# Channel attention followed by a channel mix on one core: token stripes of four per partition, held stores, and the xk mix one step later

## The chip, the cores and the metric

The kernel runs on one core of a Trainium2 chip. The time is device microseconds (us) from one launch: the median of 11 runs of the kernel before is 508.24 us, the runs lie between 506.58 and 510.48 us. One more execution was recorded by the profiler; the views below are of that one.

The engines are named as in the profile: PE multiplies matrices, PEld loads its weights, DVE and ACT work element by element, POOL here mostly issues the casting DMAs, SP issues the other DMAs. In the trace each engine works through its instructions in the order of the program (only the weight loads of PE run ahead) and waits on semaphores for the others.

## The reference, cut to what matters

```
# B, N, C = 4, 6208, 256; d_ff = 1024; float32 in and out
qn = q / (norm(q, axis=1) + 1e-6);  kn = k / (norm(k, axis=1) + 1e-6)
a  = softmax(kn^T @ qn / tau)                # 256 x 256 for each batch
x  = v @ a                                   # 6208 x 256 for each batch
x_prev = x one token earlier (zeros before the first token)
xk = mu_k * x + (1 - mu_k) * x_prev
xr = mu_r * x + (1 - mu_r) * x_prev
out = sigmoid(xr @ w_r) * (relu(xk @ w_k) ** 2 @ w_v)
```

## The kernel before, in words

**Blocks.** Each batch has 12 blocks of M = 512 tokens (S = 4 slabs of P = 128), and 64 tokens left over; the four leftovers make one last small block. So there are 48 full blocks, numbered 0 to 47 over all batches, and block 48. Everything after `x` is kept transposed, channels on the partitions and tokens along the free axis: `xT` is 128 x 2 x 513 (two channel halves, 512 tokens, and one column ahead of them with the token before).

**Start.** q and k of batch 0 are read in 13 groups of float32 by DMAs from SP (`group_load`, L113), cast and multiplied (`cov_first`, L171) while they come in. Then the softmax of batch 0 follows, block 0 of v is transposed by PE (`v_transpose_pe`, L374), and `x_first` (L412) makes the first `xT`.

**Main loop** (L709 on). For block index i the loop runs eight steps j = 0 to 7. In one pass it does the upward product of block i+1 (`up`, L507: one of eight pieces in each step, two matmuls and a Relu on ACT that leaves `kr`), the squares `kk = kr*kr` on DVE (`square`, L521: pieces 0 to 3 in one instruction at j = 4, pieces 4 and 5 at j = 6, pieces 6 and 7 at j = 0 of the next pass), the downward product of block i (`down`, L529), its end (`finish`, L549: tanh on ACT, then a DVE product into `res`, for slabs 0 to 3 at j = 3, 5, 7 and 1), and it prepares block i+2: `x_half` at j = 0 and 2 (PE product, ACT cast into `xT`), `mix_delta` at j = 3, the two halves of `xk` at j = 4 and 5, and, for block i+1, the two halves of `xr` at j = 0 and 2 (`mix`, L495).

Within a step the order is: finish, one softmax piece, up, square, down, x_half and mixes, transposes, one unit of the next batch, one of its additions. There is no scheduler: this order is the order on every engine.

**The next batch.** Beside the blocks, the covariance of the following batch is built in units (`unit`, L650): a PE product and, for two units at a time, squares on ACT, added up on DVE by `pairs_add` and `quad_add` (L229 and L233, lines L231, L235, L247). There are six units in a block up to i = 7, then four or five, and none in the last 14 blocks. An addition is taken from the queue at j = 1, 6 or 7. When a batch is complete its softmax runs as a chain of pieces, one in each step (L348): `norms` sums with PE (L279), then `roots`, `pow2` on POOL, and `invert` (L307: four DVE instructions).

**DMAs.** v is read by POOL as bfloat16 (`v_load`, L360), six blocks ahead; apart from blocks 1 and 2 partition p gets tokens p, 128+p, 256+p and 384+p, in four runs of 1 KB. From block 4 on SP transposes it (`v_transpose`, L367), five blocks ahead. `res` (three buffers) is stored by SP when slab 3 is finished (L561), again in runs of 1 KB.

The lines about `xk`, word for word:

```
                if j == 3:
                    mix_delta(n)
                if j in (4, 5):
                    mix(n, "xk", int(j > 4))
```

Of the kernel before, what the change touches and what calls it, by code (L numbers as in the profile page):

```python
# [18 lines left out]
def kernel(  # L19
# [40 lines left out]
    half = const.tile([P, 4], F32, name="half")  # L60
    vT0 = const.tile([P, 2, M + 1], BF16, name="vT0")

# [16 lines left out]
    st_ps = {}  # L79
    adds = []  # L80
    sums = {}
    now = [0]
# [30 lines left out]
    def group_load(b, g):  # L113
        rows, n = rows_of(b, g)
        if b == 0:
            t_f = []
            for i, t in enumerate((q, k)):
                f = pq.tile([P, S, C], F32, name=f"f{i}", tag=f"f{i}", bufs=6)
                (nc.sync if g else nc.scalar).dma_start(f[:rows, :n], qk_src(t, b, g))  # L119
                t_f.append(f)  # L120
            groups[b, g] = tuple(t_f)
        else:
            qk = pq.tile([P, S, 2, C], BF16, name="qk", tag="qk", bufs=5)
            groups[b, g] = (qk,)
            for i, t in enumerate((q, k)):
                nc.gpsimd.dma_start(rows_at(qk, b, g, i)[:rows, :n], qk_src(t, b, g))  # L126
# [79 lines left out]
    def unit_square(b, g, s):  # L206

        rows, n = rows_of(b, g)
        if s % 2:
            return  # L210
        qk = groups[b, g][0]
        if n == 1:
            t = sums[b, "left"] = pq.tile([P, 1, 2 * C], BF16, name="sq", tag="sq1", bufs=2)
            nc.scalar.activation(t[:rows], qk[:rows].rearrange("p s i c -> p s (i c)")[:, :1], AF.Square)
            return
        if s == 0:
            sums[b, g] = pq.tile([P, S, 2 * C], BF16, name="sq4", tag=f"f{g % 2}", bufs=6)
        t = sums[b, g]
        to = t[:, s:s + 2].rearrange("p s (i c) -> p i s c", i=2)
        if apart(b, g):  # L220
            nc.scalar.activation(to, qk.rearrange("p s i c -> p (s i c)").rearrange(
                "p (i s c) -> p i s c", i=2, s=S)[:, :, s:s + 2], AF.Square)
        else:
            nc.scalar.activation(t[:, s:s + 2], qk[:, s:s + 2].rearrange("p s i c -> p s (i c)"), AF.Square)  # L224
        if s == 2:
            adds.append((now[0] + 2, b, lambda: pairs_add(b, g)))
            adds.append((now[0] + 3, b, lambda: quad_add(b, g)))
# [38 lines left out]
    def softmax_pieces(b):  # L266
# [70 lines left out]

        def weigh(ih):
            nc.scalar.activation(a_sb[:, b, ih, :], e_sb[:, ih], AF.Copy, scale=sm[:, ih:ih + 1])

# [11 lines left out]
    NBLK = len(blocks)  # L352
    L1 = L + 1
    xl = const.tile([P, 2, B, L1], BF16, name="xl")
    st = {}
# [4 lines left out]
    def v_load(i):  # L360
        b, t = blocks[i]
        v_bf = p2.tile([P, S, C], BF16, name="v_bf", tag="v_bf", bufs=6)
        nc.gpsimd.dma_start(v_bf, v[b, t * M:(t + 1) * M, :].rearrange(  # L363
            "(p s) c -> p s c" if i in (1, 2) else "(s p) c -> p s c", p=P))
        st[i, "v"] = v_bf
# [8 lines left out]
    def v_transpose_pe(i, evac):  # L374

        v_bf = st.pop((i, "v"))
        vT_ps = ps.tile([P, S, 2, P], BF16, name="vT_ps", tag="kT_ps", bufs=3)
        for s in range(S):
            for h in range(2):
                nc.tensor.transpose(vT_ps[:, s, h], v_bf[:, s, h * P:(h + 1) * P], ident)  # L380

        if i == 0:
            return lambda: evac(vT0[:, :, 1:].rearrange("c h (s p) -> c s h p", s=S), vT_ps)
        vT = p2.tile([P, S, 2, P], BF16, name="vT", tag="vT", bufs=5)
        st[i, "vT"] = vT
        if i == 3:
            return lambda: evac(vT, vT_ps)
        flat = vT.rearrange("c s h p -> c (s h p)")
        st[i, "vT"] = flat.rearrange("c (h s p) -> c s h p", h=2, s=S)
        return lambda: evac(flat.rearrange("c (h p s) -> c h p s", h=2, s=S),  # L390
                            vT_ps.rearrange("c s h p -> c h p s"))

    def x_half(i, dh):
        b, t = blocks[i]
        if dh == 0:
            xT = p2.tile([P, 2, M + 1], BF16, name="xT", tag="xT", bufs=3)
            st[i, "x"] = xT
            if t == 0:
                nc.vector.memset(xT[:, :, 0:1], 0.0)
            else:  # L400
                nc.scalar.copy(xT[:, :, 0:1], st[i - 1, "x"][:, :, M:M + 1])
        xT = st[i, "x"]
        vT = st[i, "vT"]
        xT_ps = ps.tile([P, M], F32, name="xT_ps", tag="xT_ps", bufs=2)
        for ih in range(2):
            nc.tensor.matmul(xT_ps, a_sb[:, b, ih, dh * P:(dh + 1) * P], vT[:, :, ih, :],  # L406
                             start=ih == 0, stop=ih == 1)
        nc.scalar.copy(xT[:, dh, 1:], xT_ps)  # L408

    H = M // 2  # L410

    def x_first():  # L412

        mix_tiles(0)
        xT = p2.tile([P, 2, M + 1], BF16, name="xT", tag="xT", bufs=3)
        st[0, "x"] = xT
        dv = st[0, "d"]
        pairs = st[0, "ps"] = []

        def difference(a):  # L420
            c = slice(a * H, (a + 1) * H)
            nc.vector.tensor_tensor(dv[:, :, c], vT0[:, :, a * H + 1:(a + 1) * H + 1], vT0[:, :, c], op=OP.subtract)

        def product(a, ih):
            if ih == 0:
                pairs.append([ps.tile([P, 2, H], F32, name="x_ps", tag=tag, bufs=bufs)
                              for tag, bufs in ((("vr_ps", 2), ("vr_ps", 2)), (("s_ps", 1), ("xT_ps", 2)))[a]])
            for t, src in zip(pairs[a], (vT0[:, ih, a * H + 1:(a + 1) * H + 1], dv[:, ih, a * H:(a + 1) * H])):
                for dh in range(2):
                    nc.tensor.matmul(t[:, dh], a_sb[:, 0, ih, dh * P:(dh + 1) * P], src,  # L430
                                     start=ih == 0 and dh == 0, stop=ih == 1, skip_group_check=True)
            if ih:
                for dh in (0, 1) if a == 0 else (slice(0, 2),):
                    nc.scalar.copy(xT[:, dh, a * H + 1:(a + 1) * H + 1], pairs[a][0][:, dh])
        return difference, product

    def mix_first(key, a, dh):

        c = slice(a * H, (a + 1) * H)
        m = less[:, dh:dh + 1] if key == "xk" else less[:, 2 + dh:3 + dh]  # L440
        nc.vector.scalar_tensor_tensor(st[0, key][:, dh, c], st[0, "ps"][a][1][:, dh], m,
                                       st[0, "x"][:, dh, a * H + 1:(a + 1) * H + 1], op0=OP.mult, op1=OP.add)

# [14 lines left out]
    def left_x(b):  # L458
# [18 lines left out]
        return go, go2  # L477

    def mix_tiles(i):
        st[i, "d"] = p2.tile([P, 2, M], BF16, name="delta", tag="delta", bufs=2)  # L480
# [3 lines left out]
    def mix_delta(i):  # L484
        mix_tiles(i)
        delta = st[i, "d"]
        if i < NBLK - 1:
            xT = st[i, "x"]
            nc.vector.tensor_tensor(delta, xT[:, :, 1:], xT[:, :, :M], op=OP.subtract)  # L489
        else:  # L490
# [4 lines left out]
    def mix(i, key, dh):  # L495
        mu = mu_k_t if key == "xk" else mu_r_t
        o = st[i, key]
        if i < NBLK - 1:
            nc.vector.scalar_tensor_tensor(o[:, dh], st[i, "d"][:, dh], mu[:, dh:dh + 1],  # L499
                                           st[i, "x"][:, dh, :M], op0=OP.mult, op1=OP.add)  # L500
        else:
# [27 lines left out]
    def down(i, j):  # L529
# [5 lines left out]
        if j == 0:  # L535
            st[i, "res"] = p2.tile([P, S, D], F32, name="res", tag="res", bufs=3)
        if h == 0:
# [11 lines left out]
    def finish(i, s):  # L549
# [7 lines left out]
        b, t = blocks[i]  # L557
        dst = out[b, t * M:(t + 1) * M, :].rearrange("(s p) c -> p s c", p=P)
        if i < NBLK - 2:
            if s == S - 1:  # L560
                nc.sync.dma_start(dst, res)  # L561
        elif s % 2:
# [3 lines left out]
    def last_block(i):  # L566
# [3 lines left out]
        SL = B * L // P  # L570
        res = p2.tile([P, S, D], F32, name="res", tag="res", bufs=3)
        r_ps = ps.tile([P, SL, D], F32, name="r_ps", tag="s_ps")
# [25 lines left out]
    nc.vector.memset(fill, 1.0)  # L598
    nc.vector.memset(vT0[:, :, 0:1], 0.0)

# [46 lines left out]
    NORMS = 13  # L647
    holds = [0]

    def unit(ahead=2):  # L650
# [58 lines left out]
    for i in range(-2, NBLK - 1):  # L709
        for j in range(8):  # L710
# [7 lines left out]
            if chain:  # L718
                piece = chain[0]
                if len(chain) == NORMS and any(e[1] == holds[0] for e in adds):  # L720
                    piece = None
# [20 lines left out]
            if 0 < i + 2 < NBLK:  # L742
# [4 lines left out]
                if j == 3:  # L747
                    mix_delta(n)
                if j in (4, 5):
                    mix(n, "xk", int(j > 4))  # L750

# [24 lines left out]
            if j in slots and pos["mm"] < len(units):  # L776
                unit()
            if adds and adds[0][0] <= now[0] and (j in (1, 6, 7) or adds[0][1] == holds[0] and chain):
                next_add()
            now[0] += 1  # L780
            if i >= 0 and i % NB == 2 and j == 1 and i // NB < B:
# [41 lines left out]
```

## Time and profile before

| | |
|---|---|
| median of 11 runs | 508.24 us |
| the profiled execution | 509.51 us |
| its span, first to last instruction | 507.6 us |
| PE, DVE, ACT busy | 479.5, 431.0, 428.5 us |
| granted PE clock, mean | 0.997 |
| DMA packets, bytes moved | 132694, 83.46 MB |

A row of a group gives the line, the engine, what is written and read, shape and count, then the busy time and the mean of one instruction in ns, and the idle time of the engine just before it with what ended it. A row of the timeline gives the start and the duration in us, then the engine, the line, the shapes, "x2" where two like instructions are merged, and in brackets the idle time before it and who ended it. On DVE the next instruction can start a little before the one ahead of it is over, so the distance from start to start, called pitch here, says how long an instruction holds the queue.

### The profile page before, as it was taken

The numbers are of one execution on the slowest core, as the hardware profiler recorded it, in microseconds if no ns is written. First come the engines' busy times: TensorE is split into PE (matmuls) and PEld (weight loads), VectorE is DVE, ScalarE is ACT, GpSimd is POOL, SyncE is SP. The second block draws the span as 40 slices with busy tenths as digits, with TensorE's granted clock in tenths as the row PEclk, the third lists the DMA queues.
The fourth block names the chain that finished last, engine by engine and source line by source line (L and its number), as shares of the span: only waits on it lengthen the run. The fifth ranks groups of instructions, "written<-read, shape, count | busy, mean of one in ns | idle before, by whom it ended". The sixth has DMA issues, their size and how long they took to land.

```text
span 507.6 us, 9206 instructions
## 1 busy us (share of the span) xinstructions
PE 479.5 (94%) x3370; PEld 331.3 (65%) x3429; DVE 431.0 (85%) x788; ACT 428.5 (84%) x869; POOL 96.4 (19%) x143
## 2 busy tenths in 40 slices
PE   3578999999899999999999999999999999999996
PEld 1345667767676676676776677667666666666675
DVE  3776899999889899899889989989988787878884
ACT  5767999989899898988999898888888878888784
POOL 0044342222133322212043231200031000000000
PEclk9998999999999999999999999999999999999999
DMA  8999999999999999997699999982297753452123
GB/s 322 410 313 195 197 167 199 194 176 201 217 163 167 191 177 180 154 191 121 122 204 148 181 187 198 153 158 71 63 190 126 128 122 104 87 90 79 48 77 105
DMA packets 132694, 83.46 MB, mean 164 GB/s; under 512 B 50660, under 2 KB 125736, under 8 KB 132648
## 3 DMA queue, kind: packets, MB, share of 16 engines
q0 software_dynamic: 55824, 33.01, 49.7%
q1 hardware_dynamic: 76504, 49.59, 42.7%
q8 instruction: 27, 0.44, 0.4%
q10 hardware_dynamic: 320, 0.26, 0.2%
q14 instruction: 19, 0.16, 0.1%
HBM read 78.71 MB, written 25.43 MB: 205 GB/s over the span
## 4 chain that ended last, share of the span: by engine, by line
PE 85%; DMA 7%; DVE 5%; ACT 1%; issue 1%; SPq 0%; POOL 0%; DVEq 0%; POOLq 0%
PE vr_ps L546 32%; PE kT_ps L514 29%; PE vr_ps L542 9%; PE xT_ps L406 7%; PE s_ps L263 6%; DMA f<-in_q_dram 6%; DMA v_bf<-in_v_dram 1%; DVE kk L527 1%; DVE xk L499 1%; PE x_ps L430 1%; DVE res L556 0%; DVE xr L499 0%; ACT xT L408 0%; DVE delta L489 0%; SPq L119 0%
## 5 line engine op out<-in xcount | busy, mean ns | idle before, releaser
L519 ACT ACTIVATE kr<-kT_ps 128x512 bf16<-128x512 f32 (+1 forms) x390 | 234.9, 604 | 35.7 <-PE kT_ps L514 30.0
L546 PE MATMUL vr_ps<-w_v_sb,kk 128*128 128x256 bf16 x1536 | 230.2, 273 | 0.4
L514 PE MATMUL kT_ps<-xk,w_k_sb 128*128 128x512 bf16 (+1 forms) x722 | 217.6, 377 | 0.3 <-DVE xk L499 0.2
L546 PEld LDWEIGHTS <-kk 128*128 128x128 bf16 x1536 | 150.3, 98 | 57.3
L527 DVE TENSOR_TENSOR kk<-kr 128x2048 bf16<-128x2048 bf16 (+1 forms) x148 | 125.6, 849 | 0.2 <-ACT kr L519 0.2
L556 DVE SCALAR_TENSOR_TENSOR res<-res,vr_ps 128x256 f32<-128x256 f32 x192 | 79.7, 415 | 51.8 <-ACT res L555 51.8
L514 PEld LDWEIGHTS <-w_k_sb 128*128 128x128 bf16 x780 | 75.5, 98 | 27.5 <-issue 0.6
L555 ACT ACTIVATE res<-vr_ps 128x256 f32<-128x256 f32 x192 | 76.6, 399 | 1.3 <-PE vr_ps L546 1.3
L542 PE MATMUL vr_ps<-w_r_sb,xr 128*128 128x256 bf16 x384 | 73.3, 273 | 2.5
L408 ACT CAST xT<-xT_ps 128x512 bf16<-128x512 f32 x94 | 55.8, 594 | 19.9 <-PE xT_ps L406 19.6
L499 DVE SCALAR_TENSOR_TENSOR xk<-delta,mu_t,xT 128x512 bf16<-128x512 bf16 x94 | 69.9, 745 | 0.0
L499 DVE SCALAR_TENSOR_TENSOR xr<-delta,mu_t,xT 128x512 bf16<-128x512 bf16 x94 | 69.9, 744 | 0.0
L542 PEld LDWEIGHTS <-xr 128*128 128x128 bf16 x384 | 37.6, 98 | 44.6 <-issue 0.2
L126 POOL DMA_DIRECT2D qk<-in_q_dram x39 | 26.1, 670 | 165.0 <-ACT kr L519 141.2
L406 PE MATMUL xT_ps<-vT,a_sb 128*128 128x512 bf16 x188 | 55.9, 379 | 0.0
L263 PE MATMUL s_ps<-qk 128*128 128x256 bf16 (+1 forms) x294 | 55.8, 273 | 0.0
L224 ACT ACTIVATE sq<-qk 128x1024 bf16<-128x1024 bf16 x48 | 51.1, 1064 | 0.0
L363 POOL DMA_DIRECT2D v_bf<-in_v_dram x48 | 36.6, 766 | 51.8 <-DMA vT<-v_bf 35.8
L189 PE MATMUL s_ps<-qk 128*128 128x384 bf16 (+2 forms) x98 | 19.1, 339 | 17.2 <-ACT qk L146 15.3
L489 DVE TENSOR_TENSOR delta<-xT 128x1024 bf16<-128x1024 bf16 x47 | 32.2, 685 | 1.1 <-ACT xT L408 1.1
L263 PEld LDWEIGHTS <-qk 128*128 128x128 bf16 (+1 forms) x294 | 28.5, 98 | 5.6 <-issue 0.8
L126 POOL DMA_DIRECT2D qk<-in_k_dram x39 | 25.8, 662 | 6.6 <-DMA v_bf<-in_v_dram 2.3
(106 smaller groups left out, 251.9 us busy)
## 6 DMA issues: line engine op xcount, KB each, us to landing
out_dram<-res SPq DMA_DIRECT2D x47, 512.0 KB, 4.5
v_bf<-in_v_dram POOLq DMA_DIRECT2D x48, 256.0 KB, 8.5
qk<-in_q_dram POOLq DMA_DIRECT2D x36, 256.0 KB, 7.2
qk<-in_k_dram POOLq DMA_DIRECT2D x36, 256.0 KB, 8.7
f<-in_q_dram SPq DMA_DIRECT2D x11, 512.0 KB, 9.6
f<-in_k_dram SPq DMA_DIRECT2D x11, 512.0 KB, 10.0
vT<-v_bf SPq DMA_TRANSPOSE x44, 7.4
f<-in_q_dram SPq DMA_DIRECT2D x2, 256.0 KB, 9.0
```

What stands on the lines that cost most here:

```text
L126: nc.gpsimd.dma_start(rows_at(qk, b, g, i)[:rows, :n], qk_src(t, b, g))
L263: nc.tensor.matmul(s_ps[:, ih, :], rows_at(qk, b, g, 0)[:rows, s, ih * P:(ih + 1) * P], rows_at(qk, b, g, 1)[:rows, s, :], start=t0 and ih ...
L406: nc.tensor.matmul(xT_ps, a_sb[:, b, ih, dh * P:(dh + 1) * P], vT[:, :, ih, :], start=ih == 0, stop=ih == 1)
L408: nc.scalar.copy(xT[:, dh, 1:], xT_ps)
L499: nc.vector.scalar_tensor_tensor(o[:, dh], st[i, "d"][:, dh], mu[:, dh:dh + 1], st[i, "x"][:, dh, :M], op0=OP.mult, op1=OP.add)
L514: nc.tensor.matmul(kT_ps[:, :m], w_k_sb[:, dh, fh * P:(fh + 1) * P], xk[:, dh, :m], start=dh == 0, stop=dh == 1)
L519: nc.scalar.activation(kr, kT_ps[:, :m], AF.Relu, scale=0.5 ** 0.5)
L527: nc.vector.tensor_tensor(st[i, "kk"][:, fh // 4 * 4 + lo:fh + 1, :m], kr, kr, op=OP.mult)
L542: nc.tensor.matmul(vr_ps[:, D:], xr[:, dh, s * P:(s + 1) * P], w_r_sb[:, dh, :], start=dh == 0, stop=dh == 1)
L546: nc.tensor.matmul(vr_ps[:, :D], kk[:, fh, s * P:(s + 1) * P], w_v_sb[:, fh, :], start=fh == 0, stop=fh == 7)
L555: nc.scalar.activation(res[:, s], vr_ps[:, D:], AF.Tanh, scale=0.5)
L556: nc.vector.scalar_tensor_tensor(res[:, s], res[:, s], 1.0, vr_ps[:, :D], op0=OP.add, op1=OP.mult)
```

## The change

Tokens are dealt out differently: partition p gets the four neighbouring tokens 4p to 4p+3, so v and the stores move in runs of 4 KB, and slab s holds the tokens 4p+s. The token before one in slab s > 0 is then in slab s-1, in the same column; for slab 0 it is in slab 3, one column earlier. So `xT` becomes 128 x 2 x 4 x 129 with one extra column for each slab, the difference takes two DVE instructions (`less_one`), and the mix starts from x itself with the factor mu - 1 (`less`). `xk` is mixed at j = 5 and 6. `res` moves to the eight buffers of the tile `f0`; the squares' sums use `f1` alone. The stores of blocks 0 to 5 are kept back and issued from block 6 on, two for each block until the queue is empty (block 12). Additions are taken at j = 1, 2 and 7 (at 6 only if more than two wait), and `norms` waits for two steps after the last addition.

```diff
-        nc.gpsimd.dma_start(v_bf, v[b, t * M:(t + 1) * M, :].rearrange(
-            "(p s) c -> p s c" if i in (1, 2) else "(s p) c -> p s c", p=P))
+        nc.gpsimd.dma_start(v_bf, v[b, t * M:(t + 1) * M, :].rearrange("(p s) c -> p s c", p=P))
...
-            xT = p2.tile([P, 2, M + 1], BF16, name="xT", tag="xT", bufs=3)
+            xT = p2.tile([P, 2, S, P + 1], BF16, name="xT", tag="xT", bufs=3)
...
-        nc.scalar.copy(xT[:, dh, 1:], xT_ps)
+        nc.scalar.copy(xT[:, dh, :, 1:], slabs(xT_ps))
...
         def difference(a):
-            c = slice(a * H, (a + 1) * H)
-            nc.vector.tensor_tensor(dv[:, :, c], vT0[:, :, a * H + 1:(a + 1) * H + 1], vT0[:, :, c], op=OP.subtract)
+            less_one(dv, vT0, range(2 * a, 2 * a + 2))
...
+    def less_one(delta, x, which):
+
+        d = delta.rearrange("p h (s c) -> p h s c", c=P)
+        if 0 in which:
+            nc.vector.tensor_tensor(d[:, :, 0], x[:, :, 0, 1:], x[:, :, S - 1, :P], op=OP.subtract)
+        lo, hi = max(which[0], 1), which[-1] + 1
+        nc.vector.tensor_tensor(d[:, :, lo:hi], x[:, :, lo:hi, 1:], x[:, :, lo - 1:hi - 1, 1:], op=OP.subtract)
...
-            xT = st[i, "x"]
-            nc.vector.tensor_tensor(delta, xT[:, :, 1:], xT[:, :, :M], op=OP.subtract)
+            less_one(delta, st[i, "x"], range(S))
...
-            nc.vector.scalar_tensor_tensor(o[:, dh], st[i, "d"][:, dh], mu[:, dh:dh + 1],
-                                           st[i, "x"][:, dh, :M], op0=OP.mult, op1=OP.add)
+            m = less[:, dh:dh + 1] if key == "xk" else less[:, 2 + dh:3 + dh]
+            nc.vector.scalar_tensor_tensor(slabs(o[:, dh]), slabs(st[i, "d"][:, dh]), m,
+                                           st[i, "x"][:, dh, :, 1:], op0=OP.mult, op1=OP.add)
...
-            st[i, "res"] = p2.tile([P, S, D], F32, name="res", tag="res", bufs=3)
+            st[i, "res"] = pq.tile([P, S, D], F32, name="res", tag="f0", bufs=8)
...
-        dst = out[b, t * M:(t + 1) * M, :].rearrange("(s p) c -> p s c", p=P)
+        dst = out[b, t * M:(t + 1) * M, :].rearrange("(p s) c -> p s c", p=P)
         if i < NBLK - 2:
             if s == S - 1:
-                nc.sync.dma_start(dst, res)
+                stores.append((dst, res))
+                while len(stores) > max(0, HOLD - max(0, i - NB // 2)):
+                    nc.sync.dma_start(*stores.pop(0))
...
-                if len(chain) == NORMS and any(e[1] == holds[0] for e in adds):
+                if len(chain) == NORMS and (any(e[1] == holds[0] for e in adds) or now[0] < added[0] + 2):
...
-                if j in (4, 5):
-                    mix(n, "xk", int(j > 4))
+                if j in (5, 6):
+                    mix(n, "xk", int(j > 5))
...
-            if adds and adds[0][0] <= now[0] and (j in (1, 6, 7) or adds[0][1] == holds[0] and chain):
+            if adds and adds[0][0] <= now[0] and (j in (1, 2, 7) or j == 6 and len(adds) > 2
+                                                  or adds[0][1] == holds[0] and chain):
                 next_add()
+                added[0] = now[0]
```

More of the change, by code (lines that the diff above doesn't have):

```diff
@@ L60 @@
     half = const.tile([P, 4], F32, name="half")
-    vT0 = const.tile([P, 2, M + 1], BF16, name="vT0")
+    vT0 = const.tile([P, 2, S, P + 1], BF16, name="vT0")
     mu_rows = const.tile([4, P], F32, name="mu_rows")
@@ L80 @@
     adds = []
+    ready = set()
     sums = {}
@@ L117, in group_load @@
             for i, t in enumerate((q, k)):
-                f = pq.tile([P, S, C], F32, name=f"f{i}", tag=f"f{i}", bufs=6)
+                f = pq.tile([P, S, C], F32, name=f"f{i}", tag=f"f{i}", bufs=8 - 2 * i)
                 (nc.sync if g else nc.scalar).dma_start(f[:rows, :n], qk_src(t, b, g))
@@ L216, in unit_square @@
         if s == 0:
-            sums[b, g] = pq.tile([P, S, 2 * C], BF16, name="sq4", tag=f"f{g % 2}", bufs=6)
+            sums[b, g] = pq.tile([P, S, 2 * C], BF16, name="sq4", tag="f1", bufs=6)
         t = sums[b, g]
@@ L338, in weigh @@
         def weigh(ih):
+            ready.add((b, ih))
             nc.scalar.activation(a_sb[:, b, ih, :], e_sb[:, ih], AF.Copy, scale=sm[:, ih:ih + 1])
@@ L353 @@
     L1 = L + 1
+    HOLD = 6
+    stores = []
     xl = const.tile([P, 2, B, L1], BF16, name="xl")
@@ L382, in v_transpose_pe, with slabs @@
         if i == 0:
-            return lambda: evac(vT0[:, :, 1:].rearrange("c h (s p) -> c s h p", s=S), vT_ps)
+            return lambda: evac(vT0[:, :, :, 1:].rearrange("c h s p -> c s h p"), vT_ps)
         vT = p2.tile([P, S, 2, P], BF16, name="vT", tag="vT", bufs=5)
         st[i, "vT"] = vT
[L386 to L391, printed above, removed]
+        return lambda: evac(vT, vT_ps)
+    def slabs(a):
+        return a.rearrange("p (s c) -> p s c", c=P)
     def x_half(i, dh):
         b, t = blocks[i]
+        assert b == 0 or {(b, 0), (b, 1)} <= ready
         if dh == 0:
-            xT = p2.tile([P, 2, M + 1], BF16, name="xT", tag="xT", bufs=3)
+            xT = p2.tile([P, 2, S, P + 1], BF16, name="xT", tag="xT", bufs=3)
             st[i, "x"] = xT
             if t == 0:
-                nc.vector.memset(xT[:, :, 0:1], 0.0)
+                nc.vector.memset(xT[:, :, S - 1, 0:1], 0.0)
             else:
-                nc.scalar.copy(xT[:, :, 0:1], st[i - 1, "x"][:, :, M:M + 1])
+                nc.scalar.copy(xT[:, :, S - 1, 0:1], st[i - 1, "x"][:, :, S - 1, P:])
         xT = st[i, "x"]
@@ L414, in x_first @@
         mix_tiles(0)
-        xT = p2.tile([P, 2, M + 1], BF16, name="xT", tag="xT", bufs=3)
+        xT = p2.tile([P, 2, S, P + 1], BF16, name="xT", tag="xT", bufs=3)
         st[0, "x"] = xT
@@ L427, in product @@
                               for tag, bufs in ((("vr_ps", 2), ("vr_ps", 2)), (("s_ps", 1), ("xT_ps", 2)))[a]])
-            for t, src in zip(pairs[a], (vT0[:, ih, a * H + 1:(a + 1) * H + 1], dv[:, ih, a * H:(a + 1) * H])):
+            for t, src in zip(pairs[a], (vT0[:, ih, 2 * a:2 * a + 2, 1:], dv[:, ih, a * H:(a + 1) * H])):
                 for dh in range(2):
@@ L432, in product @@
             if ih:
-                for dh in (0, 1) if a == 0 else (slice(0, 2),):
-                    nc.scalar.copy(xT[:, dh, a * H + 1:(a + 1) * H + 1], pairs[a][0][:, dh])
+                for dh in (slice(0, 1), slice(1, 2)) if a == 0 else (slice(0, 2),):
+                    nc.scalar.copy(xT[:, dh, 2 * a:2 * a + 2, 1:],
+                                   pairs[a][0][:, dh].rearrange("p h (s c) -> p h s c", c=P))
         return difference, product
@@ L440, in mix_first @@
         m = less[:, dh:dh + 1] if key == "xk" else less[:, 2 + dh:3 + dh]
-        nc.vector.scalar_tensor_tensor(st[0, key][:, dh, c], st[0, "ps"][a][1][:, dh], m,
-                                       st[0, "x"][:, dh, a * H + 1:(a + 1) * H + 1], op0=OP.mult, op1=OP.add)
+        nc.vector.scalar_tensor_tensor(slabs(st[0, key][:, dh, c]), slabs(st[0, "ps"][a][1][:, dh]), m,
+                                       st[0, "x"][:, dh, 2 * a:2 * a + 2, 1:], op0=OP.mult, op1=OP.add)
     def up_first(fh, a):
@@ L570, in last_block @@
         SL = B * L // P
-        res = p2.tile([P, S, D], F32, name="res", tag="res", bufs=3)
+        res = pq.tile([P, S, D], F32, name="res", tag="f0", bufs=8)
         r_ps = ps.tile([P, SL, D], F32, name="r_ps", tag="s_ps")
@@ L598 @@
     nc.vector.memset(fill, 1.0)
-    nc.vector.memset(vT0[:, :, 0:1], 0.0)
+    nc.vector.memset(vT0[:, :, S - 1, 0:1], 0.0)
     def keep_warm(n):
@@ L648 @@
     holds = [0]
+    added = [0]
     def unit(ahead=2):
```

## The prediction

> **What bounds the kernel now.** I read the chain of waits first, then what PE waits for after the start, then the order on DVE in one block.
>
> ```profile
> ## 4 chain that ended last, share of the span: by engine, by line
> PE 85%; DMA 7%; DVE 5%; ACT 1%; issue 1%; SPq 0%; POOL 0%; DVEq 0%; POOLq 0%
> ```
>
> PE carries the chain; the 7% of DMA are the reading of q and k in the first 33 us and one load of v. The second view is PE's waits from 48 us to the end:
>
> ```profile
> engine line waited for: us in total, times, longest us
> PE bank L279 <- DVE sq L247: 1.4, 1, 1.4
> PE kT_ps L514 <- DVE xk L499: 0.2, 1, 0.2
> ```
>
> In 460 us PE waits 1.6 us, and never for a DMA. So little is to be had in the main loop, and the question is whether PE goes on unheld. A late block without units, on DVE:
>
> ```profile
> 430.79 0.42 DVE L556 SCALAR_TENSOR_TENSOR res<-res,vr_ps 128x256 f32<-128x256 f32 x1 [1.30 <-ACT res L555]
> 431.13 0.68 DVE L489 TENSOR_TENSOR delta<-xT 128x1024 bf16<-128x1024 bf16 x1
> 431.74 1.22 DVE L527 TENSOR_TENSOR kk<-kr 128x2048 bf16<-128x2048 bf16 x1
> 432.87 0.75 DVE L499 SCALAR_TENSOR_TENSOR xk<-delta,mu_t,xT 128x512 bf16<-128x512 bf16 x1
> 433.53 0.41 DVE L556 SCALAR_TENSOR_TENSOR res<-res,vr_ps 128x256 f32<-128x256 f32 x1
> 433.86 0.74 DVE L499 SCALAR_TENSOR_TENSOR xk<-delta,mu_t,xT 128x512 bf16<-128x512 bf16 x1
> 434.53 0.68 DVE L527 TENSOR_TENSOR kk<-kr 128x1024 bf16<-128x1024 bf16 x1
> 435.13 0.41 DVE L556 SCALAR_TENSOR_TENSOR res<-res,vr_ps 128x256 f32<-128x256 f32 x1
> ...
> 439.48 0.42 DVE L556 SCALAR_TENSOR_TENSOR res<-res,vr_ps 128x256 f32<-128x256 f32 x1 [1.30 <-ACT res L555]
> ```
>
> and PE and ACT in the same block:
>
> ```profile
> 434.58 0.59 PE L514 MATMUL kT_ps<-xk,w_k_sb 128*128 128x512 bf16 x2
> ...
> 438.57 0.59 ACT L408 CAST xT<-xT_ps 128x512 bf16<-128x512 f32 x1 [0.38 <-PE xT_ps L406]
> 439.05 0.39 ACT L555 ACTIVATE res<-vr_ps 128x256 f32<-128x256 f32 x1
> ```
>
> The second of the two matmuls at 434.58 reads the second half of xk; it starts 0.21 later (0.59 less 0.38, one matmul's length), at 434.79. That half is done at 433.86 + 0.74 = 434.60. Only 0.19 lies between. DVE is not busy here; it is tied to PE: at j = 3 it waits (1.30) for a tanh of ACT, which follows the cast of PE's x product. So there is a **loop through the block**: matmul on xk 434.79, tanh, `res` on DVE 439.48 (4.69 later), difference, square, xk, the next such matmul. It has 4.00 us for its DVE part (430.79 to 434.79) and uses 3.81 and a handover of 0.05 (in block 1, where PE did wait, xk ended at 51.88 and PE began at 51.93). The block takes 4.69 + 4.00 = 8.69.
>
> **xk a step on.** By the built order of the changed program the DVE sequence becomes: res, two differences, kk (pieces 0 to 3), res, xk, kk (pieces 4 and 5), xk. PE's order stays. The second xk is thus moved behind a square, and the whole DVE part counts by pitches from the rows above:
> - res 430.79 to 431.13: 0.34
> - differences: 0.61 before; now 256 and 768 elements. The leftovers' difference is of the first size:
>
> ```profile
> L489 DVE TENSOR_TENSOR delta<-xT 128x1024 bf16<-128x1024 bf16 x47 | 32.2, 685 | 1.1 <-ACT xT L408 1.1
> L492 DVE TENSOR_TENSOR delta<-xl 128x256 bf16<-128x256 bf16 x2 | 0.5, 288 | 0.0
> ```
>
>  288 ns less the overlap of 0.08 (0.685 long, pitch 0.61) is 0.21; 768 elements, two thirds of the way from there to 0.61, 0.47. Together 0.68.
> - kk 1.13, res 0.33, xk 0.66, kk of 1024 (434.53 to 435.13) 0.60, xk to its end 0.74.
>
> Sum 0.34 + 0.68 + 1.13 + 0.33 + 0.66 + 0.60 + 0.74 = 4.48, with the handover 4.53. Against 4.00 that is 0.53 too late, and since the loop returns through PE the lateness comes **again in every block**: 4.69 + 4.53 = 9.22 instead of 8.69. The inputs that are taken earlier are there: the second tanh ended 432.22 (wanted 432.94), piece 5 of kr at 432.88 (wanted 433.93).
>
> The room differs by phase. I took the distance from `res` at j = 3 to the second matmul of `up` for each block:
> - Blocks 36 to 47: 4.00, in block 44 4.13, so 11 x 0.53 + 0.40 = 6.2. Block 35: 4.02, and a reciprocal of the softmax (0.08) in the way: 0.6. Block 34: 4.00, and here the softmax's `invert` (in block 10 it takes from 141.59 to 142.67, 1.08) used to stand behind both xk and now stands ahead of the second: 4.53 + 1.08 - 4.00 = 1.6. Together **8.4 us**.
> - Blocks 10 and 22, with the same `invert`: 4.87, so 0.74 each; blocks 11 and 23, with the reciprocal: 4.46, so 0.15 each. Together **1.8 us**.
> - The other blocks from 12 to 33: 4.58 to 4.87. They just fit (0.05 to 0.3 left): nothing, but 0.1 more on the pitches would cost up to 20 x 0.05 = 1 us.
> - Blocks 3 to 9: 4.80 to 5.02. Additions moved to j = 2 make `res` up to 0.3 late there; still 0.1 left. Nothing.
> - Block 1: xk starts later by the square's 0.60 and 0.07: **0.7**; block 2 has 0.47 left against 0.67: **0.2**. Block 48: xk is 256 wide and ends some 0.6 ahead. Nothing.
>
> Sum of losses 8.4 + 1.8 + 0.9 = 11.1 us.
>
> **Additions and norms.** The wait of 1.4 (the gap in PE's stream is 1.6) is for the last addition of batch 1, 134.48 to 135.17, queued behind a pair of other additions. One quad-add with its accumulation (0.45 + 0.61) moves ahead of `res`. Counted through with the pitches above and the 0.9 us that blocks 1 and 2 lose, the sum ends at 135.4 where PE now would want it at 134.5: gap 0.9, **gain 0.7**. Ends: nothing to 1.6. The two-step wait does not move `norms`: PE's order is as before.
>
> **Loads and stores in runs of 4 KB.** They shorten DMA work, which no engine waits for after 48 us; what is hidden stays hidden: **0**. At the start, PE waits 1.37 us for the load of block 1 (issued 33.52, landed 40.22), behind block 0's load of 1 KB runs, and then works at half clock:
>
> ```profile
> 40.50:44.00 3.50, 3.28 (x19) 2.33 (x18) 0.95 (x4) 1.66 (x3) 1.09 (x2) 0.51 1.13 206
> ```
>
> (the third figure from the right is the granted clock). The DVE differences that the first products also need end at 41.25, the products start at 41.73; one difference is split in two now (0.2 more, half hidden by the wait for the exponentials). So 0.3 can be won if the load lands 0.5 earlier, and 1.5 more if the clock then stays up (14 matmuls of 0.21 instead of 0.11). Ends: 0.2 lost, 2.0 won. I take **0.2 won**, near the lower end, since nothing shows that the clock would stay.
>
> **Held stores.** Six stores (0.37 us of SP each) go from blocks 0 to 5 to blocks 6 to 12. Behind them on SP stand the transposes of v for five blocks on, which land in 7.4 us (median) and are wanted some 24 us later: 0. `res` of block 8 takes the buffer of block 0, whose store is issued in step 1 of pass 7; it is written first at step 3 of pass 8, 12 us later. A store lands in 4.5 us (longest 16.5): 0, at worst 4.5 for blocks 8 and 9. POOL's order is unchanged; the first-batch f buffers only grow. ACT's casts write four runs instead of one: L476 wrote 130 elements in two rows at 276 ns with no visible surcharge; 0, at worst 0.05 in each loop, 0.7 in all.
>
> **Sum.** 11.1 - 0.7 - 0.2 = 10.2 us more. The profiled execution took 509.51 (span 507.6), 1.3 above the median; so 519.7 by that execution, and 508.24 + 10.2 = **518.4** as a median. A difference of 0.3%, about 1.5 us, is what a measurement of this kernel tells from no change.
>
> **Two rules of the Trainium skill.** "VectorE: DVE Perf Modes", section "Mode 2×_1P — pack two bf16 into one 32-bit read", asks for bf16, step 1 and 4-byte alignment; the new slabs of 129 would break that at every second one. By the rule each block's differences would run at half the rate. L489, which already reads one side an odd element off, takes 685 ns, as the aligned square L527 (683); here row and rule differ, and the row decides. The section "The DRAIN you can't avoid" of the same page says that the next instruction starts only when the pipe is empty; the rows show it 0.08 before the end. By that rule the split would cost 0.15 a block, not 0.07, which is an estimate.
>
> **Rivals.**
> - *The loop does not close, and the kernel is faster.* One mechanism: the DVE part stays under the 4.00 us of the late blocks, by pitches of the new shapes of difference and xk, so PE is never held there, and the gains at the start and at `norms` remain. It decides at 4.00: above, it is slower. Then 508.24 - 0.7 to 3.6 = 505 to 507.5, say 506. For it: neither new shape is in this trace as such. Against: the square of 0.60 ahead of xk is old and measured, and alone exceeds the 0.19 left.
> - *The short runs halve DVE's rate.* Each block's differences cost 0.53 more (1024 elements at 1.14, the pitch of the square of 2048). Blocks 12 to 33 lose 0.5 each, the last 14 another 0.5: 18 us more, 536. Against: L492 has runs of 64, half as long, and no surcharge.
> - *It does nothing:* 508, where losses are some 2 us and balance the gains. This needs most of the late blocks to be free.
>
> **Chances.** Slower by the loop (514 to 523) 0.79; halved rate, or a store that holds `res` (above 523) 0.08; nothing 0.03; faster 0.10. Range 513.5 to 523: the late blocks at 0.53 less 0.25 (3.5 us less, and 1.5 of the start), or 0.1 more in all loops with a store's 1.5. Slower by over 0.3% 0.87, within 0.03, faster 0.10.
>
> **What would show it.** In the profile after, PE waits for DVE xk of `mix` some 0.5 us in each of the last 13 blocks, 7 us or more in total, and blocks there take 9.2 us. PE waits for DMA stay at nothing. If the second xk ends before PE wants it in blocks 36 to 47, the main step is wrong; if PE waits in blocks 12 to 33 too, my pitches are short.

## The result, and the profile after

The changed kernel takes 521.57 us (median of 12 runs, 520.27 to 532.46); the kernel before took 507.78 us in the 47 runs beside them. The ratio is 1.0264, with a 95% interval of 1.0242 to 1.0287: the change makes the kernel slower by 13.4 us. Forecast were 518.4 us, with a range of 513.5 to 523.

The profiled execution took 520.84 us, its span is 519.1 us at a granted clock of 0.997. The two profiled spans differ by 11.4 us. Ratios leave disturbed runs out, which puts the two medians at 521.1 and 507.7 us here; the profile of one experiment, b_v4, is of such a run and is read only beside others that show the same. The 11.4 is less than 13.4 because the profiled execution of before lies 1.8 us above 507.7 and that of after 0.2 below 521.1.

The chain of waits comes first again (share of the span, by engine):

```profile
PE 62%; DVE 21%; ACT 7%; DMA 7%; issue 2%; SPq 0%; POOL 0%; DVEq 0%; ACTq 0%; POOLq 0%
```

PE alone carried 85% before. Now DVE and ACT together carry 28%, and DMA the same 7% as before: the end is set by a chain that goes through PE, ACT and DVE in turn. PE's waits from 48 us on say where (engine, line, what it waited for; us in total, times, longest):

```profile
PE kT_ps L524 <- DVE xk L509: 8.2, 17, 1.3
PE bank L280 <- DVE sq L248: 2.7, 3, 0.9
```

Of the 1.6 us before, 10.9 have become. 17 of the waits are for `xk`, the instruction that was moved; three are for the last addition of a batch, one in each batch where there was one in all before. A late block on DVE (start, duration, line; in brackets the idle time ahead):

```profile
447.75 0.42 DVE L566 SCALAR_TENSOR_TENSOR res<-res,vr_ps 128x256 f32<-128x256 f32 x1 [1.30 <-ACT res L565]
448.08 0.29 DVE L485 TENSOR_TENSOR delta<-xT 128x256 bf16<-128x256 bf16 x1
448.29 0.56 DVE L487 TENSOR_TENSOR delta<-xT 128x768 bf16<-128x768 bf16 x1
448.76 1.22 DVE L537 TENSOR_TENSOR kk<-kr 128x2048 bf16<-128x2048 bf16 x1
449.90 0.41 DVE L566 SCALAR_TENSOR_TENSOR res<-res,vr_ps 128x256 f32<-128x256 f32 x1
450.23 0.75 DVE L509 SCALAR_TENSOR_TENSOR xk<-delta,less,xT 128x512 bf16<-128x512 bf16 x1
450.89 0.69 DVE L537 TENSOR_TENSOR kk<-kr 128x1024 bf16<-128x1024 bf16 x1
451.49 0.75 DVE L509 SCALAR_TENSOR_TENSOR xk<-delta,less,xT 128x512 bf16<-128x512 bf16 x1
```

and the matmuls of PE that read the second half of `xk`, in this block and the one ahead:

```profile
443.06 0.38 PE L524 MATMUL kT_ps<-xk,w_k_sb 128*128 128x512 bf16 x1 [0.38 <-DVE xk L509]
...
452.29 0.38 PE L524 MATMUL kT_ps<-xk,w_k_sb 128*128 128x512 bf16 x1 [0.38 <-DVE xk L509]
```

`res` starts 4.69 after the matmul (447.75 less 443.06), as before. The second `xk` ends at 451.49 + 0.75 = 452.24 and the matmul follows 0.05 later. From `res` to the matmul are 4.54 us, the block takes 9.23, and before it took 8.69. DVE still idles 1.30 ahead of `res`: it is not a busy engine that holds PE, it is the loop.

I followed the start of that matmul through all blocks, after less before. It stands at -0.45 us in block 1, at -0.24 in blocks 2 to 9, gains 0.31 in blocks 10 and 11 and 1.95 in 22 and 23, then 2.59 in block 34, 0.41 in 35 and 0.53 on average in each of 36 to 47, and ends 11.39 us behind. Between these places nothing moves.

The differences of the new shapes:

```profile
L487 DVE TENSOR_TENSOR delta<-xT 128x768 bf16<-128x768 bf16 x47 | 26.2, 557 | 0.0
L485 DVE TENSOR_TENSOR delta<-xT 128x256 bf16<-128x256 bf16 x47 | 13.5, 287 | 1.1 <-ACT xT L410 1.1
```

557 ns and 287 ns: together 0.84 us for 1024 elements, where one instruction took 0.685. In pitches that is 0.21 + 0.47 against 0.61. The rows of 129 do not slow DVE down.

### The profile page after: what moved, and what is told of

Same layout as the page of the kernel before. It is cut to its first block, busy times and chain, and to the rows that moved or that the text cites. A ratio compares the mean times of both kernels' runs of the same rounds, so it can differ in the third digit from the quotient of the medians.

```text
span 519.1 us, 9246 instructions
## 1 busy us (share of the span) xinstructions
PE 483.1 (93%) x3370; PEld 331.6 (64%) x3429; DVE 436.6 (84%) x836; ACT 429.0 (83%) x869; POOL 86.3 (17%) x143
## 2 busy tenths in 40 slices
DMA packets 96726, 83.46 MB, mean 161 GB/s; under 512 B 50660, under 2 KB 77608, under 8 KB 96680
## 4 chain that ended last, share of the span: by engine, by line
PE 62%; DVE 21%; ACT 7%; DMA 7%; issue 2%; SPq 0%; POOL 0%; DVEq 0%; ACTq 0%; POOLq 0%
PE vr_ps L556 23%; PE kT_ps L524 19%; DVE kk L537 7%; PE xT_ps L408 7%; PE vr_ps L552 7%; DVE xk L509 6%; DMA f<-in_q_dram 5%; PE s_ps L264 5%; DVE res L566 3%; ACT xT L410 2%; ACT res L565 2%; DVE delta L487 2%; ACT kr L529 2%; DMA v_bf<-in_v_dram 1%; DVE delta L485 1%
## 5 line engine op out<-in xcount | busy, mean ns | idle before, releaser
L524 PE MATMUL kT_ps<-xk,w_k_sb 128*128 128x512 bf16 (+1 forms) x722 | 220.7, 377 | 8.4 <-DVE xk L509 8.2
L509 DVE SCALAR_TENSOR_TENSOR xk<-delta,less,xT 128x512 bf16<-128x512 bf16 x94 | 70.0, 744 | 0.0
L509 DVE SCALAR_TENSOR_TENSOR xr<-delta,less,xT 128x512 bf16<-128x512 bf16 x94 | 69.9, 744 | 0.0
L367 POOL DMA_DIRECT2D v_bf<-in_v_dram x48 | 26.3, 550 | 57.7 <-DMA vT<-v_bf 48.2
L264 PEld LDWEIGHTS <-qk 128*128 128x128 bf16 (+1 forms) x294 | 28.5, 98 | 5.6 <-issue 0.6
L190 PEld LDWEIGHTS <-qk 128*128 128x128 bf16 (+1 forms) x98 | 9.9, 102 | 25.7 <-issue 14.8
## 6 DMA issues: line engine op xcount, KB each, us to landing
qk<-in_k_dram POOLq DMA_DIRECT2D x36, 256.0 KB, 10.5
```

The costliest lines, as they stand in the source:

```text
L264: nc.tensor.matmul(s_ps[:, ih, :], rows_at(qk, b, g, 0)[:rows, s, ih * P:(ih + 1) * P], rows_at(qk, b, g, 1)[:rows, s, :], start=t0 and ih ...
L509: nc.vector.scalar_tensor_tensor(slabs(o[:, dh]), slabs(st[i, "d"][:, dh]), m, st[i, "x"][:, dh, :, 1:], op0=OP.mult, op1=OP.add)
L524: nc.tensor.matmul(kT_ps[:, :m], w_k_sb[:, dh, fh * P:(fh + 1) * P], xk[:, dh, :m], start=dh == 0, stop=dh == 1)
```

## The experiments

All ratios are to the kernel before, run beside it on the same chip, with 95% intervals. The letters in the expectations are names of theories; the text beside them says which.

### The step alone, in both directions

The theory of the loop says that the place of `xk` is the main cost; its rival, that the new layout costs in itself (shapes on DVE and ACT, or the DMAs). The step was undone in the changed kernel, and done alone in the kernel before:

```diff
 # a_xk45, on the changed kernel; b_xk56 is the reverse edit on the kernel before
-                if j in (5, 6):
-                    mix(n, "xk", int(j > 5))
+                if j in (4, 5):
+                    mix(n, "xk", int(j > 4))
```

> The changed kernel with one edit undone: xk is mixed at j = 4 and 5 again, so the second half stands ahead of the square of pieces 4 and 5. Theory A (the loop through PE, tanh, DVE and xk is too long by the square's pitch): the 8.5 us of the last 14 blocks, some 1.8 us of blocks 10, 11, 22, 23 and the hold of blocks 1 and 2 go; 521.6 becomes 509 to 511.5, and late blocks take 8.7 us. Theory B (the new shapes of difference and mix, or the stripes, cost the time): stays within 2 us of 521.6. Theory C (held stores and DMA): stays as well.

> The kernel before with one edit of the change: xk is mixed at j = 5 and 6. Theory A: the DVE part of the loop is 0.34 + 0.61 + 1.13 + 0.33 + 0.66 + 0.60 + 0.74 + 0.05 = 4.46 against 4.00, so late blocks take 9.15 us; 12 x 0.46 + 1.5 in block 34 + 1.5 in blocks 10 and 22 + 0.8 in blocks 1 and 2 + 0.6 in others = 9.5 to 10 more: 517 to 518.5. Theories B and C: 508 as before.

Measured: a_xk45 511.02 us, ratio 1.0049 (1.0021 to 1.0078). b_xk56 518.97 us, ratio 1.0205 (1.0173 to 1.0238), against 508.81 of the kernel before. PE's waits in b_xk56:

```profile
PE kT_ps L514 <- DVE xk L499: 7.7, 17, 1.7
PE bank L279 <- DVE sq L247: 1.6, 1, 1.6
```

These are 17 waits as in the changed kernel, without the new stripes, the new long runs or a held store. The step alone costs 2.05% here, and undoing it takes back 2.15 of the 2.64% of the whole change (1.0264 less 1.0049). In its late blocks b_xk56 loses 0.47 each (one difference instead of two: 0.53 less 0.07); a_xk45 loses 0.04 there. What a_xk45 keeps, 0.5%, has another source. Its waits, of PE and then of ACT:

```profile
PE bank L280 <- DVE sq L248: 2.5, 3, 0.9
PE kT_ps L524 <- ACT kr L529: 2.3, 1, 2.3
```

```profile
ACT sq L222 <- DMA qk<-in_k_dram: 4.5, 1, 4.5
```

The three waits for a bank of the sums are still there, and a new one: ACT stands 4.5 us before the square of a group of q and k that has not landed, and PE stands behind ACT. After 48 us the kernel before has no wait of ACT or PE for a DMA.

### Is it the step, or what stands ahead?

Here `xk` stays in steps 5 and 6, but at step 6 its second half is issued ahead of the square of 1024, not behind it:

```diff
-                if j in (5, 6):
-                    mix(n, "xk", int(j > 5))
+                if j == 5:
+                    mix(n, "xk", 0)
...
+            if j == 6 and 0 < i + 2 < NBLK:
+                mix(i + 2, "xk", 1)
             if j > 0 and 0 <= i + 1 < NBLK:
                 square(i + 1, j - 1)
```

> The changed kernel with xk still at j = 5 and 6, but at j = 6 the second half is issued ahead of the square of pieces 4 and 5. Theory A (what counts is what stands ahead of the second xk on DVE, not the step): 0.34 + 0.68 + 1.13 + 0.33 + 0.66 + 0.74 + 0.05 = 3.93, under 4.00, so the last 13 blocks go back to 8.7 us; invert still stands ahead of the second xk in block 34 (about 1.0) and a little in 10 and 22: 510 to 512.5. If the step as such, or the layout, costs the time: 520 or more.

Measured: 511.09 us, ratio 1.0057 (1.0023 to 1.0091), and the late blocks lose 0.00 each. PE still waits for `xk` twice, 1.0 in all, and once for a transpose of v:

```profile
PE bank L280 <- DVE sq L248: 2.7, 3, 0.9
PE xT_ps L408 <- DMA vT<-v_bf: 1.5, 1, 1.5
PE kT_ps L524 <- DVE xk L509: 1.0, 2, 0.7
```

All that separates this kernel from the changed one is which comes first in each block, the second half of `xk` or a square of 0.60 us. The number of the step is not what costs; the queue ahead of the second half is.

### The start

> The kernel before with one edit: block 0 of v is read in runs of 4 KB too and put back in the order of tokens when it is copied out of PSUM. It asks what the start gained: the profile after reaches block 1's products 0.45 us earlier although xk holds them there by 0.8. Theory A (the load of block 1 no longer stands behind 512 short packets): 0.5 to 1.3 us less, 506.5 to 507.3. Rival (the start differs from run to run by where the half-clock stretch falls, not by the load): within 0.3 us of the kernel before.

The edit loads block 0 of v in 4 KB runs in the kernel before and puts its tokens back in order when PE's transposes are copied out:

```diff
-            "(p s) c -> p s c" if i in (1, 2) else "(s p) c -> p s c", p=P))
+            "(p s) c -> p s c" if i in (0, 1, 2) else "(s p) c -> p s c", p=P))
```

Measured: 507.69 us, ratio 1.0000 (0.9978 to 1.0022). Its profile has block 1 1.96 us earlier than the profile of before, and still the median is the same. The granted clock says why (stretch in us from the start of the span; the third figure from the right is the clock). Before:

```profile
36.00:40.00 4.00, 2.85 (x39) 2.33 (x38) 3.38 (x13) 2.45 (x7) 3.17 (x5) 1.00 0.94 147
40.00:44.00 4.00, 3.52 (x20) 2.58 (x22) 1.41 (x6) 1.98 (x5) 1.09 (x2) 0.57 1.12 204
```

After:

```profile
36.00:40.00 4.00, 3.12 (x41) 2.81 (x39) 2.86 (x12) 1.90 (x5) 2.60 (x5) 0.82 1.05 150
40.00:44.00 4.00, 3.66 (x28) 2.75 (x26) 2.25 (x8) 3.11 (x8) 1.06 (x2) 0.75 1.14 200
```

A stretch at half clock of 3.4 us falls in a place of its own in each: 40.5 to 43.9 us before, 38.6 to 42.0 after. In b_v0, a_xk45 and a_swap there is none at the start (1.00 in both rows), and block 1 comes about 2 us earlier. Two kernels whose starts differ in nothing, b_xk56 and the kernel before, have it at 38.7 and at 40.5 us, and a third, b_s4 (below), has none. So the execution decides, and a start read from one profile is worth up to 2 us either way.

### Holding the stores, and what waits for the DMAs

The 0.5% that a_xk45 keeps was first put down to the held stores, whose transposes on SP then come in a dense row (theory D). The stores were released at once:

```diff
-    HOLD = 6
+    HOLD = 0
```

> The changed kernel with no store held (each goes out when its block is finished); xk stays at j = 5 and 6. Theory D: the held stores cost time of their own, because a store on SP used to wait for its block and so spaced the transposes of v behind it; without them SP issues five in a row, they take the DMAs, and in executions whose start is quick PE then waits for v or for squares of q and k: 1.5 to 3 us less than the changed kernel, 518.5 to 520. If holding is free (my prediction): within 0.7 us of 521.6. If holding helps: more than 522.5.

> xk at j = 4 and 5 and no store held. With xk back alone the profile showed a wait of 4.5 us of ACT for q and k at 91 us and PE 4 us behind after it; median 511.0. Theory D: that wait goes, 508 to 509.5. If the wait came from elsewhere (the stripes, the start): 511 again.

Measured: a_hold0 523.89 us, ratio 1.0328 (1.0278 to 1.0377); a45_hold0, with `xk` in steps 4 and 5, 515.55 us, ratio 1.0161 (1.0142 to 1.0180). The gain of 1.5 to 3 us that theory D expected is in neither. With `xk` early, **holding the stores helps**: the five runs of a45_hold0 lie between 514.6 and 516.8 us, ten of the twelve of a_xk45 between 508.9 and 513.6, and the ratios differ by 1.1% (1.0161 and 1.0049). With `xk` late it is not shown: three of the six runs of a_hold0 took 520.6 to 521.2, as most runs of the changed kernel (520.3 to 521.7), the other three 526.6 to 527.7, and four of the changed kernel's twelve took 528.8 to 532.5; the intervals of the two ratios overlap. The profile of a_hold0 is of a run of 527.7 us; ACT waits 7.5 us for k in it, and PE 3.4 for ACT and 1.9 for transposes.

Then the holding alone in the kernel before (`res` in `f0`, the sums in `f1`, stores kept back as in the change), and the changed kernel without holding and with the old rule for additions:

> The kernel before with one part of the change: the stores of blocks 0 to 5 are held until block 6, res in the eight buffers of f0, the sums of squares in f1; tokens, loads and xk as before. Theory D: 1.5 to 4 us more than before, 509.5 to 512, transposes in a row from 54 us, and a wait for a DMA in PE or ACT between 60 and 100 us in executions with a quick start. If holding is free or helps: 508 or less.

> xk at j = 4 and 5, no store held, and the additions by the rule of before (j = 1, 6, 7, no two steps of waiting ahead of norms). In the changed kernel PE waits 0.9 us for the sums in each of the three batches, before 1.4 to 1.6 in the first alone. So 1.0 us less than with the new rule: 507 to 508.5. What is then left of the change is stripes, runs of 4 KB and the split difference; 0.04 us a block in the last 14 blocks (0.5 in all) is what the split should cost.

Measured: b_hold 508.19 us, ratio 1.0007 (0.9987 to 1.0027), no wait for a DMA on PE or ACT. There the holding costs nothing and wins nothing, although five transposes of v follow one another on SP from 53.9 us. a45_hold0_adds 513.71 us, ratio 1.0119 (1.0089 to 1.0149), where 507 to 508.5 were expected: ACT still waits 4.6 us for k and PE 2.2 for a transpose, and the bank wait is a single one of 1.5. The old rule gives about 0.4% back against a45_hold0; the intervals overlap a little.

So there was still to find what makes k late in the changed kernel. Two candidates were tried alone in the kernel before, with tokens in another order and the work unchanged: all of v in runs of 4 KB, or all stores.

```diff
 # b_v4
-            "(p s) c -> p s c" if i in (1, 2) else "(s p) c -> p s c", p=P))
+            "(p s) c -> p s c", p=P))
 # b_s4
-        dst = out[b, t * M:(t + 1) * M, :].rearrange("(s p) c -> p s c", p=P)
+        dst = out[b, t * M:(t + 1) * M, :].rearrange("(p s) c -> p s c", p=P)
```

> The kernel before with every block of v loaded in 4 KB runs, and nothing else: the tokens of the blocks that are transposed by DMA are then in another order, so the output is a rearranged one, with the same amount of work. Theory V (the long runs of v make the loads of q and k late): ScalarE's square waits 3 to 6 us for qk between blocks 4 and 8, and the time is 510 to 513 us. Theory S (it is the long runs of the stores) and theory H (it is neither, but how the queues fall in an execution): no such wait, 507 to 509 us.

> The kernel before with the blocks' results stored in 4 KB runs, and nothing else: rows of the output change places, the work is the same. Theory S: transposes and loads behind such a store are late, ScalarE or TensorE waits 2 us or more for qk or vT between blocks 4 and 8, 510 to 513 us. Theories V and H: nothing of it, 507 to 509 us.

Measured: **b_v4** has a ratio of 1.0152 (1.0086 to 1.0219, from three of its six runs; all six lie between 512.1 and 521.5 us), some 7.7 us on 508.53; **b_s4** takes 507.09 us, ratio 0.9975 (0.9951 to 0.9999). The long runs of v cost, and more than expected; those of the stores do not. The waits of b_v4, of PE and then of ACT and POOL:

```profile
PE xT_ps L405 <- DMA vT<-v_bf: 5.7, 3, 4.4
PE kT_ps L513 <- ACT kr L518: 2.8, 1, 2.8
```

```profile
ACT sq L221 <- DMA qk<-in_k_dram: 4.9, 1, 4.9
```

```profile
POOL qk L126 <- DMA v_bf<-in_v_dram: 11.5, 2, 11.1
```

The last row says how k comes late: POOL stands 11.1 us before it can issue a load of k, until a load of v is in. The profile of a_xk45 has the same: POOL waits 10.0 us for a load of v, issues a load of k at 86.58 us, and ACT, free at 86.5, gets its k at 91.0. The longest such wait is 4.4 to 4.6 us in a45_n4 (below) and b_hold, and 1.8 in the kernel before. b_hold and a_xk45 are a pair to look at the DMAs themselves, both with stores held (the last two figures are the time that DMA packets took, as a share of the time of 16 engines, which passes 1 where the times of packets overlap, and the GB/s moved). b_hold:

```profile
64.00:80.00 16.00, 15.89 (x116) 11.28 (x116) 15.86 (x29) 14.44 (x29) 4.72 (x8) 1.00 1.39 137
```

a_xk45:

```profile
64.00:80.00 16.00, 16.00 (x117) 11.17 (x115) 15.18 (x29) 14.47 (x29) 4.29 (x8) 1.00 1.37 100
80.00:96.00 16.00, 13.51 (x89) 8.88 (x87) 11.78 (x23) 11.24 (x24) 3.39 (x7) 0.93 1.17 147
```

From 64 to 80 us the DMA engines are as full in one as in the other (1.39 and 1.37) and move 137 GB/s in one, 100 in the other. In the next stretch PE of a_xk45 loses 2.5 us (13.51 busy), its clock drops to 0.93, and ACT has its gap. One such pair does not make it the long runs, though: a45_n4 has them too, and moves 147 at 1.36 in this stretch. The comparison without held stores is clearer: the kernel before, b_xk56, b_v0 and b_s4, with v in short runs, move 157 to 203 GB/s in it at 1.21 to 1.25; b_v4, a_hold0, a45_hold0 and a45_hold0_adds, with v in long runs, 124 to 134 at 1.23 to 1.25. In all of them the stretch holds transposes of v; why they and the loads get on worse when v comes in long runs is not settled. A last kernel was to show it from the other side, with v in four DMAs of 1 KB runs each in the changed layout:

```diff
-        nc.gpsimd.dma_start(v_bf, v[b, t * M:(t + 1) * M, :].rearrange("(p s) c -> p s c", p=P))
+        src = v[b, t * M:(t + 1) * M, :].rearrange("(p s) c -> p s c", p=P)
+        for s in range(S):
+            nc.gpsimd.dma_start(v_bf[:, s], src[:, s])
```

> The changed kernel with xk in steps 4 and 5 again, and each block of v loaded by four DMAs of a quarter in 1 KB runs, in place of one in 4 KB runs; stores held as in the change. Theory V: the square's wait for qk (4.5 us in a_xk45) goes or falls under 1.5 us, and the time to 507.5 to 509.5 us, ratio 1.000 to 1.002. Theories S and H: the wait stays and the ratio with it, 1.004 to 1.007. Four DMAs instead of one also put 1.6 us more of issuing on GpSimd for each block, which was waiting for more than that.

Measured: 516.65 us, ratio 1.0159 (1.0126 to 1.0192), slower than with one DMA. It settles nothing: between blocks 4 and 8 there is indeed no loss, but blocks 2 and 3 now lose 2.6 and 3.7 us, with ACT waiting 5.6 us for k. Four DMAs for each block of v instead of one stand in POOL's queue, a second change beside the length of the runs.

### The norms

```diff
-                if len(chain) == NORMS and (any(e[1] == holds[0] for e in adds) or now[0] < added[0] + 2):
+                if len(chain) == NORMS and (any(e[1] == holds[0] for e in adds) or now[0] < added[0] + 4):
```

> The changed kernel with xk mixed in steps 4 and 5 again, and the norms held back four steps behind the last addition instead of two. Theory N (the norms' term): TensorE's three waits for a bank of the sums (2.5 us in all in a_xk45, 0.9 each) shrink to under 0.5 us in all, the time falls by 1 to 2.5 us, from a ratio of 1.005 to 1.000 to 1.003. Rival: the weights are only late elsewhere, the waits for the bank go and TensorE waits as long for xT or for the softmax; ratio 1.004 to 1.007. Neither touches the wait for qk between blocks 4 and 8, if it comes.

Measured: 510.79 us, ratio 1.0036 (1.0002 to 1.0071). All of PE's waits from 48 us on:

```profile
PE xT_ps L408 <- ACT a_sb L341: 0.7, 2, 0.3
PE kT_ps L524 <- DVE xk L509: 0.2, 1, 0.2
```

The 2.5 us for a bank are gone and 0.7 have come for the later weights, 1.8 won by the waits. The times of a45_n4 and a_xk45 cannot be told apart (1.0036 and 1.0049, intervals overlapping): its runs lie between 507.11 and 515.29 us, and the profiled one, 507.61, has no wait for a DMA. The stall behind the DMAs, then, is not in every execution.

No kernel here beats the kernel before by more than the measurement can tell; b_s4 comes nearest, and is not the reference's order of rows.

## Why the prediction was right, and where it was off

**The loop: right in mechanism, place and size.** Forecast were blocks of 9.22 us and 8.4 us lost in the last 14; measured 9.23, and 8.5 (2.59 + 0.41 + 6.38 for blocks 36 to 47, less 0.9 of the norms in block 34). The sign to look for, PE waiting for `xk` 7 us or more in all, is there with 8.2. b_xk56 and a_swap show that it is the cause. The pitches taken for the split difference, 0.21 and 0.47, are those measured (448.08 to 448.29 to 448.76). Blocks 12 to 21 and 24 to 33 lose nothing, as forecast.

**The norms: the term that was mis-sized.** "Gain 0.7" was worked out for batch 1 alone. There it held: PE waits 0.9 instead of 1.4, and blocks 10 and 11 lose 0.31 net, near the forecast 0.89 less 0.7. But the new rules for additions and norms make the same gap of 0.9 in batches 2 and 3, in which before PE did not wait at all; blocks 22 and 23 together, and block 34, show it (1.95 where 0.89 was forecast, 2.59 where 1.6 was). With the old rules, in a45_hold0_adds, there is a single wait again, of 1.5. So the term is not 0.7 won, it is 1.3 lost by the waits (2.7 less 1.4). The change was counted at one of three like places only; the other two stood in the trace with no wait, and were not recounted.

**Loads and stores "0": wrong for the loads of v.** The step that failed is "they shorten DMA work, which no engine waits for". The packets did fall (132694 to 96726), and the stores are free (b_s4). But the loads of v in long runs cost 1.5% when put alone into the kernel before. And it was not so that no engine waited: PE did not, but POOL, which issues the loads, did, by the kernel before's own view:

```profile
POOL v_bf L363 <- DMA vT<-v_bf: 35.8, 4, 12.2
```

The 7.4 us in which a transpose lands, against the 24 that there was time for, is a median over the whole run: of the three issued between 64 and 90 us it is 23.2, and the longest took 24.8. Hardly any of that slack was left in this stretch, already before the change. With `xk` early the changed kernel is 1.6% slower without held stores (a45_hold0) and 0.5% with them (a_xk45): the prediction put both terms at nothing, and holding the stores covers most of what the loads cost. Of the 0.5%, some 2.5 us, the norms make 1.3 and the split difference about 0.5 by the profile; the wait for k that a_xk45 shows in its profile, and not all executions have, fits the rest. In the profile of after itself PE waits for no DMA.

**The start.** 0.2 won was taken; that profile has 1.1 won (0.45 in block 1, with 0.7 lost there to the square), but by the place of a half-clock stretch that changes from run to run. No run shows a gain of the long loads there; b_v0, which has the long load of block 0, is at 1.0000.

**The sum.** By the profiles: 10.2, and 2.0 for the norms (1.3 + 0.7), less the 0.9 by which the start came out better, is 11.3 against the measured 11.4. The medians differ by more, 13.4. That the profile of before lies 1.8 us above the median that is compared, and that of after 0.2 below, makes up for the rest; how much of that is the start and how much a wait for DMAs in runs that were not profiled is open.

**The rivals.** "The loop does not close" decided at 4.00 us of DVE; it measured 4.49, so it is out. "The short runs halve DVE's rate" is out: the two differences take 557 and 287 ns. So the 4-byte alignment that the page "VectorE: DVE Perf Modes" of the Trainium skill asks for (section "Mode 2×_1P — pack two bf16 into one 32-bit read") is no price of this change: slabs that begin at an odd element run at the aligned rate here. The other rule, on the drain (section "The DRAIN you can't avoid" of the same page), was only half read: the section adds that a next instruction that is not held starts earlier. The rows fit that: the second difference starts 0.21 after the first, whose length is 0.29.

## What to carry to other kernels

When an instruction is moved down a queue, do not ask whether its engine is full; find the loop that it closes through the other engines, and compare the room in it (0.19 us here) with what now stands ahead (0.60): if it does not fit, the difference comes back in every round. Recount a gain at every place of the same kind, those that had no wait too. And long DMA runs with fewer packets are no proof of an easier queue: test each stream by itself, since one change can cover for another. A median over a run says little about the stretch in which the queues are full.

## What was not expected of the hardware

The DMA engines can be as full and move clearly less: without held stores, from 64 to 80 us, 124 to 134 GB/s with v in long runs against 157 to 203 in short ones, at a share of 1.21 to 1.25 in all eight profiles. From 48 to 64 us, where the first transposes of v are issued (from 53.5 to 55 us on), it was the long runs that did better: 207 at 1.13 against 197 to 200 at 1.27 or 1.28. A load of 550 ns of issuing on POOL, shorter than the 766 ns of the short runs, came with slower landings in the profile of after: 10.0 us for v instead of 8.5 (medians), and for k 10.5 instead of 8.7. These are medians over the run; of the loads issued between 64 and 90 us, v took 20.7 us and k 21.7 in a45_hold0, where the kernel before has 13.9 and 12.6. The half-clock stretch of 3.4 us in the first 44 us differs between executions: two kernels with the same start have it 1.8 us apart, and others have none.
